# Loads of resident weights moved to another DMA queue, and one load moved behind two others

## The chip, the cores and the metric

The kernel runs on one core of a Trainium2 chip. The metric is the device time of one execution in microseconds (us). TensorE (PE in the profile) multiplies matrices; VectorE (DVE), ScalarE (ACT) and GpSimd (POOL) work on tiles; SyncE (SP) issues DMAs. A DMA can be issued by SP or by ScalarE, and stands in the program of the engine that issues it: what comes before it there has been issued before it. In the profile the transfers of SP are on the queue q1 and those of ScalarE on q10; the same 16 DMA engines carry both.

## What is computed

Three parts follow on one another, all in float32, on 8 x 576 = 4608 tokens:

```
q_s = softmax(q, over head_dim);  k_s = softmax(k, over seq)
x = q_s @ (k_s^T @ v)              # 8 batches, 8 heads, 64 wide -> x is [4608, 512]
h = x @ w_in;  g = h * sigmoid(h);                 x = g @ w_out     # first MLP, 512 -> 2048 -> 512
h = x @ w_in2; g = h * clip(h + 3, 0, 6) / 6;      out = g @ w_out2  # second MLP
```

## The kernel before

A product of float32 accuracy is made of three matmuls of split operands (a high part and a rest). Most products are also made by a scheme with seven products of half-size blocks instead of eight, so the weights are kept as seven operands, each with its high part and its rest. Such a prepared pair of weight columns is a tile of 1792 KB. It is made once, stored to DRAM in `wd`, and loaded from there by `fill` (line 277).

Tokens go in 9 blocks of 512 (NB), the hidden dimension of 2048 in 8 pairs of 128 columns (NC), so an MLP has 72 steps (PER). There are three long stages:

- **Attention and first MLP**, steps 0 to 71 (`first_cycle`, `cycle`). Weights of w_in come through a ring of two tiles, `ring`. In the last step `keep_in(2, 4, 4)` (line 760) asks for pairs 2 and 3 of the second w_in.
- **Products with the second w_in**, steps 72 to 143 (`step_in`, about 5 us each). All eight pairs stay in SBUF: pairs 0 and 1 in the ring, 2 and 3 in one pool, 4 to 7 in another. `keep_in(4, NC, 6)` (line 1239) asks for pairs 4 and 5 before the first of these steps; `slot` (line 906) asks for 6 and 7 in the steps 0 and 2. All of these tiles are `kin` in the profile. Right behind `keep_in`, `feed()` (line 1245) lets ScalarE issue the load of `st`, raw words of the second w_out, which line 127 (ScalarE) reads in the second of these steps. During these steps the second w_out is prepared, one pair a block.
- **Products with the second w_out**, 72 steps (`step_out`, line 1077 for its matmuls).

The order of the work on each engine is that of the program: it is written out by hand (`manual_schedule`), with no planner.

A step k of the second stage ends with g: `gate` on ScalarE (line 838), `gated` on VectorE (line 845), and the store of the tile g to DRAM, `gd`, on SP's queue (line 852). There are three buffers of g, so `gated` of step k waits until the store of step k - 3 has landed:

```
        x["g"] = g_p.tile([P, 2, TB], F32, tag="gs", name="g2")
    ...
        nc.sync.dma_start(out=gd[u][:, k % 2], in_=x["g"])
```

In the last block of this stage (k = 64 to 71) `last_block(p)` is called at the end of each step: for p = 0 it asks for the first two tiles gt of g (`load_g`, line 939, two steps' g in each), for p > 0 it calls `load_out(p - 1)`, which loads pair p - 1 of the second w_out into the place of the w_in pair that was used up (tiles `ring` for pairs 0 and 1, `kout` for the rest). `load_out(7)` comes after the last step (line 1251). Two steps of the third stage follow, then `load_g(2)`, `load_g(3)` and the forming of operands from g (`make_g`: lines 951, 976, 978); later tiles gt are asked for and formed inside `step_out`. The last load of a pair, of step 7 in the third stage, is so far issued ahead of `load_g(2)`.

Of the kernel before, what the change touches and what calls it, by code (L numbers as in the profile page):

```python
# [29 lines left out]
NC = NF // 2  # L30
# [5 lines left out]
def attention_two_mlps(ctx: ExitStack, tc: tile.TileContext, kqT, kv5, qn, w1, w2, out):  # L36
    nc = tc.nc
# [26 lines left out]
    def f32(ap):  # L64
        return ap.bitcast(F32)
# [91 lines left out]
    wd = {}  # L157
# [80 lines left out]
    def split_out(m, p, get_w):  # L238
        def high():
            wo[m, p] = (  # L240
                w_pool[p].tile([P, 2 * DM], F32R, tag=f"a{p}", name="woh"),
                w_pool[(p - 1) % 9].tile([P, 2 * DM], F32R, tag=f"b{(p - 1) % 9}", name="wol"),
            )
            nc.scalar.copy(wo[m, p][0], get_w())

        def low():
            h, l = wo[m, p]
            nc.vector.tensor_tensor(out=l, in0=get_w(), in1=f32(h), op=ALU.subtract)

        return [(0, high), (1.2, low)]  # L250
# [23 lines left out]
        m, t, p = place(g)  # L274
        fill(ring_tile(g), m, p)

    def fill(r, m, p):
        nc.sync.dma_start(out=f32(r).rearrange("p h s n -> p (h s n)"), in_=wd[m, p])


    un = {}
# [304 lines left out]
    second_in = {}  # L586
    WI = {1: 1, 2: 2, 3: 6, 4: 0, 5: 3, 6: 4, 7: 5}

    def place(g):
        m, r = divmod(g, PER)  # L590
        t, p = divmod(r, NC)
        return m, t, p
# [36 lines left out]
    def layer_out(g, n):  # L629

        m, t, p = place(g)
        j, c = divmod(n, KC)
        if p == 0 and n == 0:
            acc[m, t] = [ps_y.tile([P, 512], F32, tag=f"y{k}", name=f"y{k}") for k in range(KC)]
        y = acc[m, t][c]
        start, stop = p == 0 and j == 0, p == NC - 1 and j == 1
        sl = slice(c * P, (c + 1) * P)
        if whole(g):
            w = raw_out[p][:, j * DM:(j + 1) * DM]
            nc.tensor.matmul(y, lhsT=w[:, sl], rhs=gs[g, j], start=start, stop=stop)  # L640
        else:
            wh, wl = (w[:, j * DM:(j + 1) * DM] for w in wo[m, p])
            gh, gl = gs[g, j][:, 0], gs[g, j][:, 1]
            mm3(y, wh[:, sl], wl[:, sl], gh, gl, start, stop)
        if stop:
            put(m, t, c, y)
# [69 lines left out]
    def cycle(g):  # L716
        A, B_, C = (banks[k] for k in "ABC")
        lo, hi = slice(0, HT), slice(HT, TB)
        m, t, p = place(g)
        n = m * NB + t  # L720
        last = p == NC - 1
        G = lambda k: layer_out(g - 1, k)
        late = g >= LATE
        early = n == 1 and NC - 4 <= p < NC - 2

        cast_out = split_out(0, p, lambda: raw_out[p])

        def side(k):

            run(8 * g + k)  # L730
            if n == 1:
                if early and k == 2:
                    pre.append(prepare_in(p + 2))
                if k < 2:
                    cast_out[k][1]()
                for i in {0: (3, 5), 1: (6,)}.get(k, ()):
                    if len(pre) and p in (NC - 3, NC - 2):
                        pre[0][i][1]()
                        if i == 6:
                            pre.pop(0)  # L740
                if early and k in (2, 3, 5, 6):
                    pre[-1][{2: 0, 3: 1, 5: 2, 6: 4}[k]][1]()
            if late and g > LATE and k < 4:
                pump({NC - 1: (1.2, 0.8, 0.8, 0), 0: (1.2, 1.2, 1.2, 0.7)}.get(p, (2.4, 1.2, 1.2, 0.7))[k], keep=k > 0)
            if p == NC - 2 and k in (6, 7):
                sums_x(n + 1, k - 6)
            if last:
                for i in {1: (1,), 3: (5,), 4: (6, 2), 5: (3,), 6: (7,), 7: (4,)}.get(k, ()):
                    operand_x(n + 1, i)

        if g == LATE:
            attn.close()
            m2_p.append(stack("m2", 1, right, side="right"))
            stream.extend((1, q, 0) for q in range(NC))
            feed(2)
            steps.extend(chain([second(q, 0) for q in range(NC)]))
        if g == PER - 1:
            pump(99)
            right.close()
            keep_in(2, 4, 4)  # L760
        product(g, 1, A[:, lo], True)
        nc.scalar.copy(B_[:, lo], A[:, lo])
        product(g, 5, C[:, lo], True)
        s5 = z_p.tile([P, HT], F32, tag="s5", name="s5")
        nc.scalar.copy(s5, C[:, lo])
        side(0)
        G(0)
        G(1)
        product(g, 6, B_[:, lo], False)
        s2 = z_p.tile([P, HT], F32, tag="s2", name="s2")  # L770
        nc.vector.tensor_tensor(out=s2, in0=B_[:, lo], in1=s5, op=ALU.add)  # L771
        side(1)
        product(g, 2, A[:, lo], False)
        product(g, 3, A[:, hi], False)
        G(2)
        nc.vector.tensor_tensor(out=A[:, hi], in0=A[:, hi], in1=s2, op=ALU.add)  # L776
        ba, bc = bend(g, 0, A), bend(g, 1, B_)
        next(ba)
        side(2)
        product(g, 7, B_[:, lo], False)  # L780
        nc.vector.tensor_tensor(out=B_[:, hi], in0=B_[:, lo], in1=s5, op=ALU.add)
        next(ba)
        G(3)
        side(3)
        G(4)
        product(g, 4, B_[:, lo], False)
        if not early:
            load_w(g + 2)
        for _ in ba:
            pass  # L790
        next(bc)
        next(bc)
        side(4)
        G(5)
        for _ in bc:
            pass
        side(5)
        G(6)
        side(6)
        G(7)  # L800
        side(7)
# [2 lines left out]
    kept, early, mid = (ctx.enter_context(ExitStack()) for _ in range(3))  # L804
    kept_p = {}

    def keep_in(a, b, now):
        q = stack(f"kept{a}", 1, kept, side="right")
        for p in range(a, b):
            kept_p[p] = q  # L810
            second_in[p] = q.tile([P, 2, 7, 2 * P], F32R, tag=f"k{p}", name="kin")
            if p < now:
                fill(second_in[p], 1, p)

    gd = {}
    a2 = {}
# [70 lines left out]
    def beside(k):  # L887
        t, p = divmod(k, NC)
        n = NB + t + 1
        if p == 0 and t < NB - 1:  # L890
            c = [c[1] for c in second(t, 1, add=nc.gpsimd)]
            mag, floor, shift, sign, low, sum_0, sum_1, high_0, low_0, high_1, low_1, keep_0, keep_1 = c
            f = lambda i, part: (lambda: operand_x(n, i, part))
            more = [feed] * (t < NC - 1)
            a2["table"] = [
                [lambda: load_y(n)] * (t > 0) + a2.pop("over", []), [], [mag], [floor], [shift], [sign],
                [low, sum_0, sum_1, f(1, 0)], [f(1, 1), f(2, 0), lambda: sums_x(n, 0, nc.gpsimd)],
                [f(2, 1), lambda: sums_x(n, 1, nc.gpsimd)], [high_1], [low_1, f(3, 0)],
                [f(3, 1), f(5, 0), keep_1, *more], [f(5, 1), f(7, 0)], [f(7, 1), f(4, 0)],
                [f(6, 0), f(4, 1), f(6, 1), high_0], [low_0],  # L900
            ]
            a2["over"] = [keep_0]

        def slot(i):
            if k in (0, 2) and i == 1:
                fill(second_in[6 + k // 2], 1, 6 + k // 2)
            if t < NB - 1:
                for fn in a2["table"][2 * p + i]:
                    fn()
            else:  # L910
                if i:
                    last_block(p)
                for fn in ahead_of_out().get(2 * p + i, ()):
                    fn()

        return slot
# [3 lines left out]
    def load_out(p):  # L920
        if p < 2:
            r = ring_tile(2 * PER + p)
        else:
            r = kept_p[p].tile([P, 2, 7, 2 * P], F32R, tag=f"k{p}", name="kout")
        second_out[p] = r
        fill(r, 2, p)

    out_p = {}
    ORDER = [*range(NB - 2), NB - 1, NB - 2]
# [3 lines left out]
    def load_g(u):  # L933
        t, h = divmod(u, NC // 2)
        if u % 3 < 2:
            raws[u] = out_p["a"].tile([P, 2, 2, TB], F32, tag="gt", name="gt", bufs=2)
        else:
            raws[u] = out_p["b"].tile([P, 2, 2, TB], F32, tag="gt", name="gt")
        nc.sync.dma_start(out=raws[u], in_=gd[ORDER[t] * (NC // 2) + h])
# [40 lines left out]
    def make_g(q):  # L980
        if q % 2 == 0:
            for j in range(4):
                sums_g(q // 2, j)
        form_g(q, 0, 0)
        form_g(q, 1, 0)
        form_g(q, 0, 1)
        form_g(q, 1, 1)
# [165 lines left out]
    with tc.manual_schedule():  # L1153
# [82 lines left out]
            layer_out(PER - 1, k)  # L1236
        weights_1.close()
        load_y(NB + 1)
        keep_in(4, NC, 6)
        sums.close()  # L1240
        up["p"] = stack("in_ps", 1, mid, space=bass.MemoryType.PSUM)
        raw_bufs[0] = 1
# [5 lines left out]
        for k in range(PER):  # L1248
            step_in(k, beside(k))
        step_in(PER, lambda i: None)  # L1250
        load_out(NC - 1)
        mid.close()
        up["p"] = stack("out_ps", 1, mid, space=bass.MemoryType.PSUM)
        step_out(0)
# [2 lines left out]
        out_p["b"] = stack("out_b", 1, mid)  # L1257
        load_g(2)
        load_g(3)
        make_g(2)  # L1260
        make_g(3)
        for q in range(2, PER):
# [55 lines left out]
```

## Time and profile before

| | us |
|---|---|
| median of 3 runs | 1669.71 |
| lowest and highest run | 1666.25, 1675.86 |
| the profiled execution | 1680.23 |
| its span, first to last instruction | 1678.4 |

The profile is of that one execution. TensorE is busy for 96% of the span, VectorE for 71%, ScalarE for 46%, GpSimd for 15%. The mean granted clock of TensorE is 0.99 of full speed. q1 moves 323.49 MB, q10 61.35 MB. In a row of a timeline the first number is the start and the second the length, both in us; a bracket at the end has the idle time of the engine ahead of the instruction and what ended it. A row of an engine with a q (SPq, ACTq) is the issue of a DMA, and its length includes what the issue waited for if several are merged; "x3" are three instructions.

### The profile page before, as it was taken

What the parts mean: (1) busy time and instruction counts of PE and PEld (TensorE: products, weight loads), DVE (VectorE), ACT (ScalarE), POOL (GpSimd) and SP (SyncE); (2) the same over time, 40 slices, a digit from 0 to 9 for tenths busy, and PEclk for the clock granted to TensorE, in tenths of its full rate; (3) what the DMA queues carried; (4) which work ended last, traced back from release to release, by engine and by line L of the source; (5) the groups of instructions that cost most, each with busy time, mean ns of one, the idle gap of its engine ahead of it and who ended that gap; (6) DMA issues with size and microseconds to landing.
All of it is one profiled execution on the core that took longest, in us unless ns stands there. A gap on an engine that the chain in (4) does not pass through costs nothing. (4 is left out here: it accounts for less than half of the span.)

```text
span 1678.4 us, 28093 instructions
## 1 busy us (share of the span) xinstructions
PE 1617.6 (96%) x11112; PEld 1461.3 (87%) x11112; DVE 1194.6 (71%) x1910; ACT 767.0 (46%) x1383; POOL 249.4 (15%) x188
## 2 busy tenths in 40 slices
PE   6999999999999999999999899999999899999998
PEld 4445878888889898988789899999999899999998
DVE  7998686575656647568777577777776587778875
ACT  5544555454444545344444455555554343343332
POOL 2211232222222222200000122222220000000000
PEclk9999999999999999999999999999999899999999
DMA  8589979999899999858888955555558833333332
GB/s 297 188 283 287 241 222 240 264 274 262 211 286 263 246 261 263 232 211 319 298 317 330 367 198 200 195 208 205 201 204 335 331 144 126 127 126 126 126 127 75
DMA packets 90107, 386.62 MB, mean 230 GB/s; under 512 B 21880, under 2 KB 25976, under 8 KB 67960
## 3 DMA queue, kind: packets, MB, share of 16 engines
q1 hardware_dynamic: 77272, 323.49, 61.2%
q10 hardware_dynamic: 12704, 61.35, 10.6%
q8 instruction: 87, 1.43, 0.3%
q14 instruction: 44, 0.36, 0.1%
HBM read 283.90 MB, written 100.90 MB: 229 GB/s over the span
## 5 line engine op out<-in xcount | busy, mean ns | idle before, releaser
L1077 PE MATMUL M<-kout,f 128*128 128x256 f32 x2268 | 273.0, 282 | 2.4 <-DVE f L978 1.9
L1077 PEld LDWEIGHTS M<-kout,f 128*128 128x128 f32 x2268 | 271.4, 190 | 3.2 <-DVE f L978 2.3
L77 PE MATMUL y<-gs,woh 128*128 128x512 f32 x512 | 205.9, 402 | 2.8 <-ACT gs L73 2.8
L78 PE MATMUL y<-gs,woh 128*128 128x512 f32 x512 | 203.4, 397 | 0.2 <-DVE gs L74 0.2
L79 PE MATMUL y<-gs,wol 128*128 128x512 f32 x512 | 201.2, 393 | 0.0
L976 ACT CAST f<-gt 128x1024 fp32r<-128x1024 f32 x72 | 75.6, 1050 | 180.5 <-DVE gt L951 98.9
L77 PE MATMUL B<-o,ring 128*128 128x256 f32 x492 | 142.7, 290 | 14.3 <-DVE s L771 7.6
L74 DVE TENSOR_TENSOR gs<-g,gs 128x512 fp32r<-128x512 f32 x128 | 102.4, 800 | 70.8 <-ACT gs L73 70.0
L79 PE MATMUL B<-o,ring 128*128 128x256 f32 x492 | 139.8, 284 | 0.0
L78 PE MATMUL B<-o,ring 128*128 128x256 f32 x492 | 139.7, 284 | 0.0
L77 PE MATMUL A<-op,ring 128*128 128x256 f32 x444 | 127.2, 286 | 2.2 <-DMA ring<-wd 2.2
L78 PE MATMUL A<-op,ring 128*128 128x256 f32 x444 | 126.0, 284 | 2.4 <-DVE op L578 2.4
L79 PE MATMUL A<-op,ring 128*128 128x256 f32 x444 | 125.8, 283 | 0.0
L619 ACT ACTIVATE g<-A 128x512 f32<-128x512 f32 x72 | 43.0, 598 | 176.3 <-DVE A L776 165.4
L77 PEld LDWEIGHTS B<-o,ring 128*128 128x128 f32 x492 | 93.8, 191 | 31.6 <-DVE s L771 11.8
L79 PEld LDWEIGHTS y<-gs,wol 128*128 128x128 f32 x512 | 97.2, 190 | 21.9
L73 ACT CAST gs<-g 128x512 fp32r<-128x512 f32 x128 | 79.2, 619 | 79.7 <-DVE g L621 78.8
L77 PEld LDWEIGHTS y<-gs,woh 128*128 128x128 f32 x512 | 97.8, 191 | 15.8 <-ACT gs L73 3.0
L978 DVE TENSOR_TENSOR f<-gt,f 128x1024 fp32r<-128x1024 f32 x72 | 88.0, 1222 | 32.2 <-ACT f L976 30.9
L77 PE MATMUL B<-o,kin 128*128 128x256 f32 x324 | 94.5, 292 | 14.5 <-DVE B L862 14.4
L78 PEld LDWEIGHTS y<-gs,woh 128*128 128x128 f32 x512 | 98.0, 192 | 9.4 <-DVE gs L74 0.5
L845 DVE SCALAR_TENSOR_TENSOR g<-a,A 128x512 f32<-128x512 f32 x72 | 49.5, 688 | 75.8 <-ACT a L838 60.8
(224 smaller groups left out, 4219.7 us busy)
## 6 DMA issues: line engine op xcount, KB each, us to landing
ring<-wd SPq DMA_DIRECT2D x66, 1792.0 KB, 10.6
gd<-g SPq DMA_DIRECT2D x72, 512.0 KB, 3.4
gt<-gd SPq DMA_DIRECT2D x36, 1024.0 KB, 4.9
st<-w_dram SPq DMA_DIRECT2D x16, 1024.0 KB, 6.2
st<-w_dram ACTq DMA_DIRECT2D x16, 1024.0 KB, 8.6
wd<-r ACTq DMA_DIRECT2D x16, 1024.0 KB, 5.6
ev<-kv_dram SPq DMA_DIRECT2D x24, 640.0 KB, 9.2
wd<-ring ACTq DMA_DIRECT2D x8, 1792.0 KB, 9.8
```

The lines of the kernel that those rows point to most:

```text
L73: nc.scalar.copy(hi, src)
L74: nc.vector.tensor_tensor(out=lo, in0=src, in1=f32(hi), op=ALU.subtract)
L77: nc.tensor.matmul(o, lhsT=wh, rhs=xh, start=start, stop=False, **kw)
L78: nc.tensor.matmul(o, lhsT=wh, rhs=xl, start=False, stop=False, **kw)
L79: nc.tensor.matmul(o, lhsT=wl, rhs=xh, start=False, stop=stop, **kw)
L619: nc.scalar.activation(out=a, in_=hb, func=AF.Tanh, scale=0.5)
L845: nc.vector.scalar_tensor_tensor(out=x["g"][:, j], in0=x["a", j], scalar=1.0, in1=x["AB"[j]], op0=ALU.min, op1=ALU.mult)
L976: nc.scalar.copy(o[0], src)
L978: nc.vector.tensor_tensor(out=o[1], in0=src, in1=f32(o[0]), op=ALU.subtract)
L1077: nc.tensor.matmul(M[:, h * 2 * P:(h + 1) * 2 * P], lhsT=a, rhs=b, start=p == 0 and h == 0 and e == 0, stop=p == NC - 1 and e == 2, skip_g ...
```

## The change

The fills of pairs 4 to 7 of the second w_in and all fills of the second w_out are issued by ScalarE instead of SP. Pairs 2 and 3 stay with SP, and so do the stores of g, the loads gt and the ring's loads of the first MLP. The load of the last w_out pair moves from behind the last w_in step to behind `load_g(2)` and `load_g(3)`.

```diff
-    def fill(r, m, p):
-        nc.sync.dma_start(out=f32(r).rearrange("p h s n -> p (h s n)"), in_=wd[m, p])
+    def fill(r, m, p, by=nc.sync):
+        by.dma_start(out=f32(r).rearrange("p h s n -> p (h s n)"), in_=wd[m, p])
...
-            keep_in(2, 4, 4)
+            keep_in(2, 4, 4, nc.sync)
...
-    def keep_in(a, b, now):
+    def keep_in(a, b, now, by):
...
-                fill(second_in[p], 1, p)
+                fill(second_in[p], 1, p, by)
...
             if k in (0, 2) and i == 1:
-                fill(second_in[6 + k // 2], 1, 6 + k // 2)
+                fill(second_in[6 + k // 2], 1, 6 + k // 2, nc.scalar)
...
         second_out[p] = r
-        fill(r, 2, p)
+        fill(r, 2, p, nc.scalar)
...
-        keep_in(4, NC, 6)
+        keep_in(4, NC, 6, nc.scalar)
...
         step_in(PER, lambda i: None)
-        load_out(NC - 1)
         mid.close()
...
         load_g(2)
         load_g(3)
+        load_out(NC - 1)
         make_g(2)
```

## Rows read from the trace of the kernel before

**Rows 1.** The page: busy us, share of the span, instructions of each engine.
```profile
PE 1617.6 (96%) x11112; PEld 1461.3 (87%) x11112; DVE 1194.6 (71%) x1910; ACT 767.0 (46%) x1383; POOL 249.4 (15%) x188
```

**Rows 2.** Waits, whole span: who waited for what; us in total, times, longest.
```profile
DVE g L845 <- DMA gd<-g: 15.1, 5, 7.4
```

**Rows 3.** Timeline of TensorE near 940, 959, 1306, 1320 and 1331.
```profile
940.10 0.28 PE L77 MATMUL B<-o,kin 128*128 128x256 f32 x1
...
959.16 0.58 PE L77 MATMUL B<-o,kin 128*128 128x256 f32 x1 [6.25 <-DVE B L862]
...
1306.15 0.58 PE L77 MATMUL B<-o,kin 128*128 128x256 f32 x1 [3.66 <-DVE B L862]
...
1319.62 10.10 PE L1077 MATMUL M<-kout,f 128*128 128x256 f32 x84
1330.22 0.50 PE L1077 MATMUL M<-kout,f 128*128 128x256 f32 x2 [0.51 <-ACT f L976]
...
1331.73 1.58 PE L1077 MATMUL M<-kout,f 128*128 128x256 f32 x8 [1.01 <-DVE f L978]
```

**Rows 4.** Stretches: length, busy us by engine, TensorE's clock, DMA share, GB/s.
```profile
960.00:965.00 5.00, 5.00 (x29) 5.00 (x29) 2.60 (x7) 3.10 (x5) 0.00 (x0) 0.59 0.36 145
...
1296.00:1300.00 4.00, 4.00 (x36) 4.00 (x36) 2.40 (x5) 1.90 (x4) 0.00 (x0) 1.00 1.01 430
...
1306.00:1312.00 6.00, 5.85 (x27) 5.85 (x28) 3.39 (x6) 0.69 (x1) 0.00 (x0) 0.50 1.01 428
...
1332.00:1336.00 4.00, 4.00 (x22) 3.90 (x22) 3.93 (x6) 1.08 (x2) 0.00 (x0) 0.59 0.34 72
```

**Rows 5.** Timeline of SP (issues of DMAs), 930 to 947.
```profile
930.99 2.58 SPq L278 DMA_DIRECT2D kin<-wd  x3
941.35 5.20 SPq L852 DMA_DIRECT2D gd<-g  x2
```

**Rows 6.** Timeline of ScalarE, 929 to 939.
```profile
929.52 0.33 ACTq L101 DMA_DIRECT2D st<-w_dram  x1
930.28 0.36 ACT L824 COPY B<-A 128x256 f32<-128x256 f32 x1 [0.17 <-PE A L79]
...
936.73 1.16 ACT L127 ACTIVATE w<-st 128x1024 f32<-128x1024 f32 x1 [1.64 <-DMA st<-w_dram]
938.17 0.36 ACT L824 COPY B<-A 128x256 f32<-128x256 f32 x1 [0.28 <-PE A L79]
```

**Rows 7.** Timeline of VectorE near 957, 1304 and 1328.
```profile
956.87 0.69 DVE L845 SCALAR_TENSOR_TENSOR g<-a,A 128x512 f32<-128x512 f32 x1 [7.39 <-DMA gd<-g]
...
1304.46 0.69 DVE L845 SCALAR_TENSOR_TENSOR g<-a,A 128x512 f32<-128x512 f32 x1 [2.84 <-DMA gd<-g]
...
1327.67 0.69 DVE L951 TENSOR_TENSOR tg<-gt 128x512 f32<-128x512 f32 x1 [6.02 <-DMA gt<-gd]
```

**Rows 8.** DMA near 969, 970:974, 989, 143: issues to landing; queues' packets, MB, share.
```profile
st<-w_dram ACTq DMA_DIRECT2D x1, 1024.0 KB, 8.6
...
gd<-g SPq DMA_DIRECT2D x1, 512.0 KB, 8.6
...
q10 hardware_dynamic: 213, 1.07, 104.6%
...
gd<-g SPq DMA_DIRECT2D x1, 512.0 KB, 2.6
...
q10 hardware_dynamic: 33, 0.47, 50.2%
```

**Rows 9.** DMA, the issue at 932.03: KB, us to landing.
```profile
kin<-wd SPq DMA_DIRECT2D x1, 1792.0 KB, 19.2
```

**Rows 10.** Timeline of ScalarE, last block, step of 1293.
```profile
1293.03 0.69 ACT L838 ACTIVATE a<-B,half 128x512 f32<-128x512 f32 x1
```

**Rows 11.** Timeline of SP, last block and the step behind it.
```profile
1294.47 0.32 SPq L852 DMA_DIRECT2D gd<-g  x1
...
1314.18 19.84 SPq L939 DMA_DIRECT2D gt<-gd  x4
```

## The prediction

> **What bounds the kernel now.** I read the page first: TensorE is busy for 1617.6 us of a span of 1678.4 [rows 1], so nothing but its idle time and its slow stretches can be won, and 61 us is all the idle time there is. The view of the waits comes second. In it the reader looks for a wait whose releaser the change touches: VectorE's line 845, which writes g, waited 15.1 us in five waits for the stores gd<-g [rows 2]. These stores share SP's queue with the 1792 KB weight loads. The third view is TensorE's timeline, read for its brackets. In the second MLP three places matter, and VectorE's timeline tells what each waits for:
>
> - **Start of the second MLP.** Idle 6.25 us until 959.16 [rows 3]. VectorE waited 7.39 us for a store of g [rows 7], issued at 941.35 behind three loads of resident pairs [rows 5].
> - **End of its last block.** Idle 3.66 us until 1306.15 [rows 3]; VectorE waited 2.84 us for a store [rows 7].
> - **Fifth step of the output product.** Idle 0.51 and 1.01 us near 1331 [rows 3], because the tile gt came only at 1327.67 [rows 7].
>
> After each, the view by stretches shows the granted clock at 0.5 of full speed, the 1.2 GHz level. A matmul then takes twice as long, so a stretch at half speed loses half its length. In 960 to 965 the mean of 0.59 makes 4.1 us at half and 2.05 us lost; in 1306 to 1312, 5.85 busy us at 0.50 lose 2.9; in 1332 to 1336, 0.59 makes 3.28 us at half and 1.6 lost [rows 4]. So the places cost 8.3, 6.6 and 3.1 us, 18 us together: the scope of a change that removes all three.
>
> **The change part by part.** Its intent works only if a transfer on ScalarE's queue does not hold one on SP's queue. The trace shows such a pair in each block: by 968.7 ScalarE has issued a load of st (1024 KB, 8.6 us to landing), and at 969.7 SP issues a store of g. This store took 8.6 us to land too; one with no neighbour, near 989.6, took 2.6. In 970.5 to 974.5 ScalarE's queue q10 had all the busy time of the 16 DMA engines, 104.6%, with the store waiting on q1 [rows 8]. So the transfers were served in the order of issue, over both queues. Against that stands one stretch, 142.6 to 144.8, where two loads of equal size, one on each queue, shared: q10 had 50.2% [rows 8]. I take order of issue, as the case with a store of g behind loads is the one that matters here, and keep sharing as a rival.
>
> The Trainium skill says otherwise (DMA: Bandwidth & Descriptors, section "Queues, rings and completion order"): each DMA engine takes turns between the queues that have work, a packet at a time. By that rule the stores of g would pass the loads. The stretch at 142.6 agrees with it, the one at 970.5 does not; the sum by it is the first rival's.
>
> *Start of the second MLP.* Two loads of kin (pairs 4 and 5) move to ScalarE's queue, and in ScalarE's program they stand ahead of feed(), which loads st. In the trace st is issued at 929.52, ahead of all, and line 127, which reads it, starts at 936.73 after an idle 1.64 us that st's landing ended [rows 6]. Behind line 127 in ScalarE's program stands the copy of line 824, at 938.17 [rows 6], and a product of TensorE needs that copy, at 940.10 [rows 3]. So TensorE hides only about 1.6 us of a later st (940.10 less the copy's end at 938.53).
>
> After the change st comes behind 2 x 1.835 MB. A load of 1792 KB at the 430 GB/s of the stretch 1296 to 1300 [rows 4] takes 4.27 us. Which transfers are served by then is the same set as before (st, yd, xr, two of kin); before, the second kin closed it, issued at 932.03 and 19.2 us later landed, at 951.2 [rows 9]. Now st closes it. If st gets ahead of xr (of st's size, 1.05 MB; at 430, 2.4 us), it lands at 948.8. Then 1.16 us for line 127, 0.36 for the copy and 0.1 for the semaphore: TensorE goes on at 950.4 to 952.8.
>
> The three DMA issues also stand ahead of the copy at 930.28. SP's issue of these three loads took 2.58 us in all [rows 5], st's 0.33 [rows 6]; two and st cost 2.05 us from 929.52, so the copy starts near 931.5 instead of 930.28. TensorE has about 0.2 us to spare there: 1.0 us lost, bounds 0 and 2.
>
> So TensorE runs dry at 941.1 and waits until 950.4 to 952.8: 9.3 to 11.7 us, I take 10.5. The old idle 6.25 goes: all of block 1 is delayed, and the stores then find the queue nearly empty. Clock cost as before. **Sum: 1.0 + 10.5 - 6.25 = +5.25 us.** Bounds: if ScalarE's queue alone were served from 931 (the yd and xr of SP held back), st would land after 8.5 + 2.4 us at 942, the gap would be 2.5 us and the sum -2.75; above, copy 2 and gap 11.7 give +7.5. I take the upper half, as the landing at 951.2 is a row for the same bytes.
>
> The loads of pairs 6 and 7 are needed at steps 6 and 7, more than 15 us later: nothing.
>
> *Last block.* Here q1 is full: 430 GB/s at a busy share of 1.01 [rows 4]. Each step issues one store of g (512 KB) and one w_out pair (1792 KB), the store first, as at 1294.47 [rows 11]. On ScalarE the pair's load will follow line 838 of the same step, which starts at 1293.03 [rows 10]; the store must still wait for that operation and for VectorE. So each load will be issued about 1.4 us ahead of the store that it followed, and in order of issue each store gets one pair more ahead of it: 4.27 us. VectorE has three g buffers and already waits for a store in the last two steps, with no cover left: **+4.27 us**. Bounds: 0, if the store still goes first; +7.7, if the waits, then in three steps, cost two more stretches at half clock (1.7 us each, as near 1334).
>
> The eight issues themselves (0.33 us each, as st's [rows 6]) fall behind line 838, where ScalarE then waits for TensorE in most steps: nothing; with that cover gone, 2.6 us.
>
> *The last pair behind the two gt loads.* SP issued the last w_out pair just ahead of four gt loads, the first at 1314.18 [rows 11]. Taking 1.835 MB from in front brings gt 4.27 us earlier, to about 1323.4. VectorE idled 6.02 us until gt came [rows 7], so its chain moves by as much and TensorE's 1.52 us of idle time and the 1.6 at half clock go: **-3.1 us**. Late next is the last pair itself, landing near 1330; it is read by the eighth step. At 5.06 us a step (two steps, 84 matmuls, in 10.10 us from 1319.62 [rows 3], the third and fourth) that is 1319.6 + 5 x 5.06 = 1345: covered by 15 us. Bounds -3.1 and 0.
>
> **Total:** 5.25 + 4.27 - 3.1 = +6.4 us on the profiled execution (1678.4 span, 1.83 around it, 1680.2), that is 1686.6. This execution was 10.5 us above the median of the runs, 1669.7; the difference carries over: **1676.1 us**, 0.4% slower. About 0.5% (8.3 us) is what can be told from no change, so it may not show.
>
> **Rivals.**
>
> - *The queues share.* Stores of g pass the loads. st is still third on its own queue: SP's 2.1 MB and ScalarE's first 2.1 MB take until 940.8, the other 1.57 MB of kin 3.65 us and st 2.4 to 4, so it lands near 947.6, and the gap is 947.6 + 1.6 - 941.1 = 8.1: +2.9 at the start. In the last block VectorE's wait of 2.84 goes but its operand from ScalarE is ready only 2.05 us sooner; with 0.38 us a step earlier and half of the clock's cost, -3.9. With -3.1: -4.1 us, **1665.6**. For it: 142.6; against: 970.5.
> - *It does what it says*, and st is not late, because the 1.64 us wait ends by another transfer than I think. Then -8.3, -3.9 and -3.1: -15.3, **1654.4**. Against it: the order of the program on ScalarE.
> - *Slower for certain.* Loads that pass the stores spread the wait at the end over three steps, and the clock falls in each: place 1288 to 1312, price 3.4 us more than my sum, +9.8, **1679.5**. It decides as soon as the clock is at half ahead of 1300. For it: near 1331 the clock fell after 1.5 us of idle time; against: the single waits may stay short.
>
> **How the numbers follow.** My forecast 0.42 (own range 1672 to 1680), sharing 0.20, all as meant 0.13, slower for certain 0.20, something else 0.05. Faster by over 0.5% (below 1661.4): 0.13 + 0.05 of sharing + 0.04 = 0.22. Slower (above 1678.1): 0.16 + 0.14 of my own + 0.03 = 0.33. Within: 0.45. The range, 1660 to 1683, takes in the upper bounds of the start and leaves out "all as meant" and little else.
>
> **What would show it.** Right: line 127 in the first block waits about 12 us or more for st; TensorE idles some 10 us near 945; the idle time near 955 for gd<-g is gone; VectorE's waits for gd<-g in the last block are longer; no wait for gt near 1327. Wrong: stores of g landing in under 6 us beside loads on q10, or a short wait at line 127.

## The result and the profile after

The changed kernel takes **1683.26 us**, the median of 8 runs (1678.83 to 1690.57). The kernel before, run beside it, takes 1675.09 (8 runs, 1666.25 to 1678.46). The ratio is 1.0061, with an interval from 1.0042 to 1.0079, which is 7.0 to 13.2 us, 10.2 in the middle (the two medians alone are 8.2 apart). So it is slower, by more than the 6.4 us of the forecast. The forecast of 1676.1 was made from the median of three runs, 1669.71; in these eight the kernel before stands 5.4 us higher, and this part of the distance between 1676.1 and 1683.26 has nothing to do with the change.

The profiled execution took 1684.22 us, its span is 1682.4. Spans differ by what happens long ahead of the change, so I cut both traces at five marks and compare the stretches. The marks are the starts of the last line 655 of the first MLP (an activation on ScalarE), of the 17th and the 64th store gd, of the first matmul of line 1077, and of the first matmul of its seventh step.

| stretch | before | after | difference |
|---|---|---|---|
| start (line 655 to 17th store) | 929.5 to 1029.9: 100.3 | 923.2 to 1029.4: 106.2 | +5.9 |
| middle (to the 64th store) | 238.8 | 238.5 | -0.3 |
| last block (to the first line 1077) | 1268.7 to 1307.6: 38.9 | 1267.8 to 1316.4: 48.6 | +9.7 |
| first six steps of the output product | 35.6 | 30.8 | -4.8 |
| rest | 335.2 | 335.3 | 0.1 |

Each is rounded by itself; from mark one to the end it is 748.9 and 759.2, **+10.3**. In the eleven kernels below and here the middle lies between 238.3 and 238.8 and the rest between 335.1 and 335.3, though the change does not touch them; the start lies between 99.7 and 100.3 in the five kernels that leave it as it was. So I take 1 us as a difference, though each figure is from one execution.

First the page of after: the engines' line and the two queues (packets, MB, share of 16 engines).

```profile
PE 1614.7 (96%) x11112; PEld 1458.1 (87%) x11112; DVE 1188.3 (71%) x1910; ACT 766.3 (46%) x1383; POOL 248.1 (15%) x188
...
q1 hardware_dynamic: 75544, 301.47, 58.5%
q10 hardware_dynamic: 14432, 83.37, 13.5%
```

TensorE's busy time is no larger than before [rows 1]. From mark one on it is 727.5 us in both, so in sum what was lost is idle time, 21.4 us before and 31.7 after. 22.0 MB went from q1 to q10: the 12 loads of 1.835 MB that changed engine.

**Start.** ScalarE's and TensorE's timelines of after near 925 and 945, and the view by stretches (length, busy us of PE, PEld, DVE, ACT, POOL, TensorE's clock, DMA share, GB/s).

```profile
923.21 1.30 ACTq L278 DMA_DIRECT2D kin<-wd  x2
924.54 0.72 ACTq L101 DMA_DIRECT2D st<-w_dram  x1
925.37 0.36 ACT L824 COPY B<-A 128x256 f32<-128x256 f32 x1 [1.57 <-PE C L79]
...
944.09 1.12 ACT L127 ACTIVATE w<-st 128x1024 f32<-128x1024 f32 x1 [13.91 <-DMA st<-w_dram]
```

```profile
925.77 0.39 PE L77 MATMUL B<-o,ring 128*128 128x256 f32 x1 [1.19 <-ACT B L824]
...
945.53 0.58 PE L77 MATMUL B<-o,kin 128*128 128x256 f32 x1 [10.20 <-ACT B L824]
```

```profile
935.00:945.00 10.00, 0.34 (x3) 0.13 (x2) 0.00 (x0) 0.91 (x1) 0.00 (x0) 0.73 1.01 427
...
945.00:950.00 5.00, 4.47 (x22) 4.47 (x23) 3.47 (x7) 1.94 (x5) 0.00 (x0) 0.53 0.55 228
```

The two loads of pairs 4 and 5 now stand ahead of st in ScalarE's program. Line 127 waits 13.91 us for st, where it waited 1.64 [rows 6]; the copy of line 824 stands behind it, and TensorE, which needs the copy, idles 1.19 and 10.20 us. Meanwhile the DMA engines are full (1.01, 427 GB/s). The clock is at half when work resumes. The wait of 7.39 us at line 845 [rows 7] and TensorE's 6.25 [rows 3] are gone.

**Last block.** TensorE's timeline, VectorE's, the stretches, and the waits of after for stores of g (us in total, times, longest).

```profile
1281.51 0.38 PE L77 MATMUL B<-o,kin 128*128 128x256 f32 x1 [2.01 <-DVE B L862]
...
1291.94 0.58 PE L77 MATMUL B<-o,kin 128*128 128x256 f32 x1 [5.26 <-DVE B L862]
...
1314.94 0.58 PE L77 MATMUL B<-o,kin 128*128 128x256 f32 x1 [4.16 <-DVE B L862]
```

```profile
1289.65 0.69 DVE L845 SCALAR_TENSOR_TENSOR g<-a,A 128x512 f32<-128x512 f32 x1 [6.93 <-DMA gd<-g]
...
1295.26 0.69 DVE L845 SCALAR_TENSOR_TENSOR g<-a,A 128x512 f32<-128x512 f32 x1 [1.58 <-DMA gd<-g]
...
1313.26 0.69 DVE L845 SCALAR_TENSOR_TENSOR g<-a,A 128x512 f32<-128x512 f32 x1 [3.34 <-DMA gd<-g]
```

```profile
1290.00:1295.00 5.00, 3.06 (x14) 3.06 (x15) 3.68 (x7) 1.89 (x4) 0.00 (x0) 0.61 0.78 328
...
1315.00:1320.00 5.00, 5.00 (x29) 5.00 (x30) 2.53 (x4) 0.69 (x1) 0.00 (x0) 0.66 0.99 420
```

```profile
DVE g L845 <- DMA gd<-g: 15.5, 5, 6.9
```

The sum of the waits for gd<-g is almost that of before, 15.5 against 15.1 us [rows 2], in as many waits. Whoever reads only this view sees no loss. The waits have moved: the one of 7.39 at the start is gone, and one of 6.93 has appeared in the middle of the last block, where before had none until 1298. Of the wait for gt [rows 7] 1.74 us are left, at 1331.02. TensorE idles 2.01, 5.26 and 4.16 us in the block, 11.4 together; before it was 3.66 [rows 3] and two of 0.76 and 0.38. The clock falls to half at 1291 and again at 1315. The whole block by the view of stretches, before and then after:

```profile
1268.70:1307.60 38.90, 34.10 (x281) 33.44 (x280) 23.68 (x44) 16.22 (x30) 0.00 (x0) 0.97 1.01 404
...
1267.80:1316.40 48.60, 36.99 (x281) 36.19 (x280) 23.68 (x45) 16.27 (x30) 0.00 (x0) 0.92 0.97 368
```

The same 281 matmuls keep TensorE busy for 36.99 us instead of 34.10. So of the 9.7 us about 2.9 are work at the lower clock and 6.8 are idle time.

Why one store takes so long is seen in the issues and in the DMA view. First ScalarE's issues of loads in after, then SP's issues: two loads gt, and two stores, each pair merged in one row:

```profile
1271.12 0.33 ACTq L278 DMA_DIRECT2D ring<-wd  x1
...
1278.34 0.33 ACTq L278 DMA_DIRECT2D ring<-wd  x1
```

```profile
1268.24 1.82 SPq L939 DMA_DIRECT2D gt<-gd  x2
...
1272.82 8.04 SPq L852 DMA_DIRECT2D gd<-g  x2
```

The store that VectorE waited for is the first of these two. A load of ScalarE's was issued 1.7 us ahead of it, another 5.5 us behind; the store had landed when line 845 went on, at 1289.65, which is 16.8 us after its issue. Ahead of it on its own queue stood the two loads gt. The queues in 1276 to 1280 (packets, MB, share):

```profile
DMA packets 152, 1.63 MB, mean 407 GB/s; under 512 B 11, under 2 KB 11, under 8 KB 11
...
q10 hardware_dynamic: 77, 1.10, 72.2%
q1 hardware_dynamic: 75, 0.52, 32.1%
```

No packet has between 512 B and 8 KB, so none is of the store, whose rows are 4 KB: q1 still sent gt, with 32% of the engines. Before, from 1273.8 to 1277, q1 had the engines to itself for these loads (1.15 MB, 104.4%). So the store of after started late because what stood ahead of it was slowed. In 1285 to 1289 it was q1's stores that shared with ScalarE's loads:

```profile
DMA packets 207, 1.72 MB, mean 429 GB/s; under 512 B 21, under 2 KB 21, under 8 KB 114
...
q10 hardware_dynamic: 106, 1.32, 77.9%
q1 hardware_dynamic: 100, 0.38, 23.2%
```

The queues sent about **as many packets each**, 106 and 100. A packet that carries data is one row of a tile: 1792 KB over 128 partitions is 14,336 bytes, 512 KB is 4,096. By the bytes these are 92 rows of the loads (1.32 MB / 14,336) and 93 of the stores (0.38 MB / 4,096); 21 packets are under 512 B and move next to nothing. With equal turns a store gets 4096 / (4096 + 14336) = 0.22 of the rate; the row says 0.23 (23.2 of 101.1).

### The profile page after: what moved, and what is told of

Same layout as the page of the kernel before. It is cut to its first block, busy times and chain, and to the rows that moved or that the text cites. A ratio compares the mean times of both kernels' runs of the same rounds, so it can differ in the third digit from the quotient of the medians.

```text
span 1682.4 us, 28087 instructions
## 1 busy us (share of the span) xinstructions
PE 1614.7 (96%) x11112; PEld 1458.1 (87%) x11112; DVE 1188.3 (71%) x1910; ACT 766.3 (46%) x1383; POOL 248.1 (15%) x188
## 4 chain that ended last, share of the span: by engine, by line
PE 58%; DMA 12%; DVE 9%; ACT 3%; issue 3%; ACTq 0%; POOL 0%; DVEq 0%; SPq 0%; POOLq 0%
PE M L1077 19%; PE y L77 4%; PE y L78 4%; PE y L79 4%; PE B L77 4%; PE B L78 3%; PE B L79 3%; PE A L77 3%; PE A L79 3%; PE A L78 3%; DMA wd<-r 3%; DMA gd<-g 3%; DMA qr<-qr 2%; DMA ring<-wd 2%; ACT a L838 1%
## 5 line engine op out<-in xcount | busy, mean ns | idle before, releaser
L74 DVE TENSOR_TENSOR gs<-g,gs 128x512 fp32r<-128x512 f32 x128 | 96.0, 750 | 71.0 <-ACT gs L73 70.1
L77 PEld LDWEIGHTS B<-o,ring 128*128 128x128 f32 x492 | 93.2, 189 | 31.8 <-DVE s L771 14.5
L73 ACT CAST gs<-g 128x512 fp32r<-128x512 f32 x128 | 79.1, 618 | 75.3 <-DVE g L621 74.5
```

The lines of the kernel that those rows point to most:

```text
L73: nc.scalar.copy(hi, src)
L74: nc.vector.tensor_tensor(out=lo, in0=src, in1=f32(hi), op=ALU.subtract)
L77: nc.tensor.matmul(o, lhsT=wh, rhs=xh, start=start, stop=False, **kw)
```

## The experiments

In the table all figures are from one profiled execution of each kernel, cut at the same marks. "Block and six steps" is the third and fourth stretch together, which is safer where a stall or its half clock lies across the mark between them. From mark one to the end, the difference to before agrees with the ratio within 3 us in every kernel but e4, where it is 5 us off.

| kernel | start | last block | six steps | block and six steps | ratio to before, interval |
|---|---|---|---|---|---|
| before | 100.3 | 38.9 | 35.6 | 74.5 | 1 |
| after | 106.2 | 48.6 | 30.8 | 79.3 | 1.0061 [1.0042, 1.0079] |
| e1_last_pair | 99.7 | 38.1 | 31.9 | 70.0 | 0.9982 [0.9960, 1.0005] |
| e2_kin_act | 106.5 | 38.9 | 35.8 | 74.6 | 1.0030 [1.0010, 1.0050] |
| e3_out_act | 100.3 | 46.6 | 31.7 | 78.4 | 1.0016 [0.9997, 1.0034] |
| e4_st_first | 99.1 | 49.1 | 30.6 | 79.6 | 0.9993 [0.9977, 1.0010] |
| e5_sp_load_first | 100.3 | 42.0 | 29.9 | 71.9 | 0.9985 [0.9967, 1.0003] |
| e6_act_load_later | 100.0 | 41.5 | 32.9 | 74.4 | 0.9993 [0.9975, 1.0011] |
| e8_small_desc | 107.3 | 37.3 | 31.8 | 69.1 | 1.0005 [0.9988, 1.0023] |
| e7_spread | 96.9 | 36.3 | 31.5 | 67.8 | 0.9923 [0.9899, 0.9947] |
| e9_mended | 95.9 | 37.2 | 31.4 | 68.5 | 0.9945 [0.9925, 0.9964] |

**One part alone: e1, e2, e3.** e1 is before with only the last pair moved:

```diff
         step_in(PER, lambda i: None)
-        load_out(NC - 1)
...
         load_g(3)
+        load_out(NC - 1)
```

> Only the last edit: the load of the last w_out pair behind load_g(2) and load_g(3), everything on SP's queue as before. My theory (the pair stood ahead of gt): the wait for gt near 1327 goes, the stage from the first matmul of the output product to its seventh step falls from 35.6 us to 31 or 32, and the whole by 3 to 5 us. Rival (gt is late for the backlog as a whole): the wait stays, no change.

VectorE's timeline of e1:

```profile
1320.40 0.69 DVE L951 TENSOR_TENSOR tg<-gt 128x512 f32<-128x512 f32 x1 [3.10 <-DMA gt<-gd]
```

The wait for gt went from 6.02 us [rows 7] to 3.10, TensorE no longer idles in the first six steps, and its clock no longer falls a second time: 31.9 instead of 35.6, -3.7. The rest of the output product stays at 335.2, so the last pair came in time for the eighth step. In the median the gain is 1.6 us, and its interval holds no change.

e2 is before with the fills of pairs 4 to 7 on ScalarE and nothing else:

```diff
-        keep_in(4, NC, 6)
+        keep_in(4, NC, 6, nc.scalar)
...
-                fill(second_in[6 + k // 2], 1, 6 + k // 2)
+                fill(second_in[6 + k // 2], 1, 6 + k // 2, nc.scalar)
```

> Only the resident pairs 4 to 7 of the second w_in on ScalarE's queue, ahead of the load of st. My theory: line 127 waits some 14 us for st as in the changed kernel, TensorE idles about 10 us near 945, and the stage from the last eviction of the first MLP to the 17th store of g takes 106 us instead of 100.3; the last block and the tail stay at 38.9 and 35.6; in all +6 us. Rival (the loss is all in the last block): no change.

ScalarE's timeline of e2, and TensorE's:

```profile
951.07 1.12 ACT L127 ACTIVATE w<-st 128x1024 f32<-128x1024 f32 x1 [14.20 <-DMA st<-w_dram]
```

```profile
952.52 0.58 PE L77 MATMUL B<-o,kin 128*128 128x256 f32 x1 [10.48 <-ACT B L824]
```

All of the start is here: 106.5 against 106.2 in after, with the same two rows; the last block is untouched. e2 is measurably slower than before, by 1.7 to 8.4 us.

e3 is before with only the fills of the second w_out on ScalarE, the last pair in its old place:

```diff
-        fill(r, 2, p)
+        fill(r, 2, p, nc.scalar)
```

> Only the loads of the w_out pairs on ScalarE's queue, the last of them still ahead of the gt loads. Order of issue (each store gets one pair more ahead of it): the last block 43 us instead of 38.9. Turns by descriptor (a store with 4096-byte descriptors gets 4096 / (4096 + 14336) = 0.22 of the DMA engines beside a pair's load with 14336-byte ones): as in the changed kernel, 48 to 49 us. Tail: 35.6 or longer, as gt is still behind the last pair. Start as before, 100.3.

The waits of e3:

```profile
DVE g L845 <- DMA gd<-g: 23.9, 8, 7.5
```

The last block takes 46.6, +7.7 of the +9.7 in after: most of the loss is here without the other two parts of the change. The wait of 7.5 is in the block, at 1280.47. The 46.6 lies between the 43 expected for order of issue and the 48 to 49 expected for turns. The six steps fall to 31.7 as well, though the last pair was not moved in the program: on q10 it no longer stands ahead of gt on q1. So the gain of the moved pair and the new queue do not add up; either alone brings nearly all of it.

**The start undone: e4.** After, but ScalarE issues st before pairs 4 and 5:

```diff
-        keep_in(4, NC, 6, nc.scalar)
+        keep_in(4, NC, 4, nc.scalar)
...
         feed()
+        for p in (4, 5):
+            fill(second_in[p], 1, p, nc.scalar)
```

> The changed kernel with the load of st issued ahead of the pairs 4 and 5, still on ScalarE's queue. Both theories: line 127 waits under 3 us. Order of issue: the first store of g is behind the pairs' loads again, VectorE waits some 7 us for it and the start takes 99 to 101 us, as before the change. Turns by descriptor: the store shares from the time it is issued, lands in 6 to 9 us instead of 15.4, and the start takes 94 to 97 us. Last block and tail as in the changed kernel, 48.6 and 30.8.

ScalarE's timeline of e4, then the issue of a store of g beside these loads (KB, us to landing):

```profile
929.53 1.14 ACT L127 ACTIVATE w<-st 128x1024 f32<-128x1024 f32 x1 [2.56 <-DMA st<-w_dram]
```

```profile
gd<-g SPq DMA_DIRECT2D x1, 512.0 KB, 12.4
```

Line 127 waits 2.56 us instead of 13.91, and the start takes 99.1 instead of 106.2. That settles the mechanism: st was late because of its place in ScalarE's program. But the store, with the pairs' loads on the other queue, still took 12.4 us, where turns had been expected to give 6 to 9, and TensorE idled 4.27 us for it. It was not alone on its own queue. The load xr that SP issued at 920.95 (KB, us to landing), and q1 in 933.5 to 937, behind the issue of the store at 933.23:

```profile
xr<-yd SPq DMA_DIRECT2D x1, 1024.0 KB, 19.2
```

```profile
DMA packets 136, 1.47 MB, mean 420 GB/s; under 512 B 6, under 2 KB 6, under 8 KB 6
...
q1 hardware_dynamic: 66, 0.52, 35.4%
```

No packet is of the store's 4 KB: q1 still sent xr, which shared the engines with the pairs' loads and landed near 940. Separate queues did not free the stores; they slowed what stood ahead of the store on its own queue. The last block stays at 49.1, as it should. The whole run shows 0.9993, some 5 us less than the stretches of this one execution would give (752.5 against 748.9); I rest only on the stretches that differ from after.

**The last block taken apart: e5, e6, e8.** In after a w_out load is issued ahead of the store of its step *and* on another queue. e5 does the first alone: before, all on SP, the load issued right ahead of the store, and the last pair as in e1.

```diff
-        if p:
-            load_out(p - 1)
...
             gate(k - 1, 1)
+            slot(2)        # load_out(p - 1) in the last block, on SP
...
```

> All loads on SP's queue; in the last block each w_out pair's load stands ahead of the store of g that it followed, and the last pair behind the gt loads. Order of issue costs what was forecast, one pair more ahead of each store: last block 43 us (38.9 before), tail 31 to 32, as on one queue nothing takes turns. If the last block takes 48 us, the queue is no matter and the order alone makes the loss of the changed kernel; if it takes 39, the order does not matter either. Start as before, 100.

VectorE's timeline of e5:

```profile
1292.84 0.69 DVE L845 SCALAR_TENSOR_TENSOR g<-a,A 128x512 f32<-128x512 f32 x1 [2.80 <-DMA gd<-g]
...
1304.01 0.69 DVE L845 SCALAR_TENSOR_TENSOR g<-a,A 128x512 f32<-128x512 f32 x1 [2.14 <-DMA gd<-g]
```

A wait of about 2 to 3 us in each of four steps (1.79, 2.80, 2.05 and 2.14), none long: TensorE idles about 1 us for each, and 2.96 at the end of the block, and the clock does not fall. 42.0, +3.1 in the block and +1.9 against e1 with the six steps; 43 was expected for order of issue.

e6 does the second alone: ScalarE issues the load, but behind the store, in the next step; the last pair as in e1.

```diff
-        fill(r, 2, p)
+        fill(r, 2, p, nc.scalar)
...
             gate(k, 0)
+        slot(3)            # load_out(p - 2) in the last block
...
```

> Start on SP as before. In the last block the loads of the w_out pairs are issued by ScalarE, but about 3 us later in the step, behind the store of g that they followed before; the last pair behind the gt loads. Order of issue alone: the last block takes 38 to 39 us, as before. Turns by descriptor: a load issued behind a store still takes 0.78 of the engines once both are in service, so stores land later than before and the last block takes 42 to 47 us. Tail 31 to 32.

The store issued at 1281.96 in e6 (KB, us to landing):

```profile
gd<-g SPq DMA_DIRECT2D x1, 512.0 KB, 9.7
```

41.5, +2.6 in the block, +4.4 against e1 with the six steps, where 1.0 of it lies (VectorE waits 6.25 us for gt again). Turns were expected to give 42 to 47, order alone 38 to 39: it lies between. The store goes ahead of its step's load here, and still takes 9.7 us beside the load of the step before, issued at 1277.88 and 11.4 us to landing; in before, with such a load ahead of it on the same queue, stores took 7.9 and 8.4.

e8 is after, with each w_out fill cut into two DMAs whose rows are 3,584 bytes instead of 14,336; order, queues and bytes are those of after, and ScalarE issues two DMAs where it issued one.

```diff
...
+        if m == 2:
+            o, i = (a.rearrange("p (a b n) -> p b a n", a=2, b=2) for a in (o, i))
+            for j in range(2):
+                by.dma_start(out=o[:, j], in_=i[:, j])
...
```

> The changed kernel with each w_out pair's load made of two DMAs of the same bytes with rows of 3584 bytes instead of 14336, so a store with rows of 4096 gets 0.53 of the engines beside it instead of 0.22. Turns by descriptor: stores of g in the last block land in 5 to 9 us instead of up to 17, and the last block takes 41 to 44 us instead of 48.6. Order of issue alone: 48 to 49 us. Start 106, tail 31, as in the changed kernel.

The queues of e8 in 1291 to 1293 (packets, MB, share), in the last block:

```profile
q1 hardware_dynamic: 107, 0.44, 53.4%
q10 hardware_dynamic: 115, 0.39, 49.0%
```

And a store of g in the same block (KB, us to landing):

```profile
gd<-g SPq DMA_DIRECT2D x1, 512.0 KB, 7.1
```

Again as many packets each, but the store's are now the larger ones (4096 / (4096 + 3584) = 0.53), and q1 gets 53.4 where it got 23.2. The last block falls from 48.6 to 37.3, below that of before and of the 41 to 44 that I expected, and the ratio from 1.0061 to 1.0005. This is the run that decides: with order, queue and bytes kept, shorter rows are worth 11.3 us. No run splits a load in two and keeps the long rows; that the rows do it, and not the splitting, is read from the shares.

**Two versions: e7 and e9.** e7 leaves everything on SP and moves loads away from the crowded places: pairs 6 and 7 of w_in one step later each, four w_out pairs in the last block instead of seven, the others behind the last store or behind the gt loads.

```diff
-            if k in (0, 2) and i == 1:
+            if k in (1, 3) and i == 1:
...
-        if p:
+        if p in (1, 2, 3):
             load_out(p - 1)
+        if p == NC - 1:
+            load_out(3)
...
-        load_out(NC - 1)
+        load_out(4)
...
         load_g(3)
+        for p in range(5, NC):
+            load_out(p)
```

> All loads on SP's queue, spread out: pair 6 of w_in is asked for after the first store of g and pair 7 after the third (steps 1 and 3 instead of 0 and 2); of the w_out pairs 0 to 2 in the last block as before, pair 3 behind its last step but one, pair 4 behind its last step, 5 to 7 behind load_g(2) and load_g(3). Both theories: with one pair less ahead of it the first store lands 4.3 us sooner: start 97 to 98.5 us instead of 100.3. In the last block no store is behind more than one pair: VectorE does not wait for gd<-g, 35 to 36 us instead of 38.9. Tail 31 to 32, if no pair comes too late (each is due 5.06 us after the one before); in all 8 to 10 us faster than before.

The waits of e7, and TensorE's timeline at the start and at the end of the last block:

```profile
DVE g L845 <- DMA gd<-g: 3.1, 2, 2.2
```

```profile
938.95 0.58 PE L77 MATMUL B<-o,kin 128*128 128x256 f32 x1 [2.96 <-ACT B L824]
...
1296.36 0.38 PE L77 MATMUL B<-o,kin 128*128 128x256 f32 x1 [1.64 <-DVE B L862]
```

The waits for stores fall from 15.1 us [rows 2] to 3.1, and none is left in the start or the last block (the two are at 970.87 and 1052.59). 1660.73 against 1675.59: 0.9923, 8.9 to 16.9 us faster than before. It has the lowest ratio here, though its interval and that of e9 overlap.

e9 is e4 with the rows of every fill on ScalarE cut as in e8:

```diff
...
+        if by is nc.scalar:
+            o, i = (a.rearrange("p (a b n) -> p b a n", a=2, b=2) for a in (o, i))
...
```

> The changed kernel with both faults mended: st asked for ahead of the pairs 4 and 5, and every load of a pair that ScalarE issues made of two DMAs with rows of 3584 bytes. Turns by descriptor: the first store of g lands in 6 to 10 us beside the pairs' loads (12.4 with rows of 14336), the start takes 96 to 98 us, the last block 37 to 38, the tail 31 to 32; in all 6 to 9 us faster than before. Order of issue in the start: 99 us there, as with st first alone.

The first store of e9, which answers to the one of 12.4 us in e4, and ScalarE's timeline:

```profile
gd<-g SPq DMA_DIRECT2D x1, 512.0 KB, 7.0
```

```profile
926.30 0.34 ACTq L101 DMA_DIRECT2D st<-w_dram  x1
926.67 3.72 ACTq L282 DMA_DIRECT2D kin<-wd  x4
```

1665.89 against 1675.84: 0.9945. With st first and short rows the change does what it says, at the start too: 95.9, no fall of the clock. The first store, issued at 941.56, does not find xr ahead of it any more: q1 had no packet from 940.6 to 945. Its price shows in the second row: four issues hold ScalarE for 3.72 us, and TensorE idles 3.22 for the copy behind them.

## Why the prediction was right in its sign and wrong in its size

**Start, +5.25: right.** Line 127 waiting for st, the copy and TensorE behind it, the vanished wait for gd<-g: each was seen. The copy cost 1.19 (1.0), the gap was 10.20 (10.5), the clock cost about what it did before (TensorE is busy for 94.2 us of the stretch, 93.9 before), and the stretch +5.9. e2 has it alone, e4 takes it away. That the gap came out so close is in part luck: it was worked out by order of issue over both queues, and in 930 to 935 of after both queues sent at once, 105 packets with 1.28 MB on q10 and 107 with 0.86 MB on q1.

**Last block, +4.27: the step that failed.** It measured +9.7 in after and +7.7 in e3. The step reads "in order of issue each store gets one pair more ahead of it: 4.27 us", and had chosen order of issue *over* sharing, one or the other. e5 has that order with nothing else, on one queue, and costs +3.1: the term by itself exists, and was put somewhat too large. What the step left out is sharing, which e6 has without the order, +2.6. Sharing was a rival of mine, but as a gain: "stores of g pass the loads". The shares above are those of turns of a packet, and the packets of a store are 3.5 times smaller (14336 / 4096), so a store beside a load is slowed, not freed. So are the loads gt with rows of 8 KB, which stand ahead of the first store on q1. Against e1, which like after has the last pair moved, block and six steps cost +1.9 in e5 and +4.4 in e6 but +9.3 with both in after: more than their sum. In after one long wait brings the clock to half in the middle of the block, at 1291; in e5 it does not fall in the block, in e6 only near its end, at 1298. e8 takes all of it back with shorter rows: block and six steps 69.1, against 70.0 in e1.

I had the numbers for this. The stretch at 142.6 [rows 8] has 33 packets with 0.47 MB, 14.2 KB each: two transfers with equal rows share equally, and this says nothing of a store with rows of 4 KB. (They were not two loads: q1's was the load ring<-wd, q10's the store wd<-ring issued at 139.14.) The rows at 970.5, where the store of g had nothing, were of a transfer that had not yet entered service; they say nothing of the share once it has. Nor was st alone ahead of it: ScalarE had issued a store wd<-r too, at 968.09. In the last block of after the first store waits behind gt, which is slowed by small turns, and then takes small turns itself. The rule of turns that I set aside (the Trainium skill, DMA: Bandwidth & Descriptors, "Queues, rings and completion order") fits the packets of both stretches, 106 to 100 and 107 to 115. What the times hang on is how much a packet carries.

**Rival "slower for certain", +9.8.** Its mark came: the clock was at half ahead of 1300, at 1291, and the +10.2 is close to its +9.8. Its course was another: two long waits of 6.93 and 3.34 us and a short one of 1.58, with the clock falling after two of them and not after all three. By the last block alone it has 4.27 + 3.4 = 7.7 where +9.7 was measured, so the close total is luck in part.

**Last pair, -3.1: right.** e1 has -3.7. After has -4.8, and the clock accounts for the 1.1 more: in before 4.6 us of the half speed from 1305.4 lie behind the mark at 1307.6 (as much as in e1), in after 2.0 of that from 1315.0 (3.4 long) behind 1316.4, and half of the difference is 1.3 us. That is time that moved into the last block, not a gain.

**Total.** 5.9 + 9.7 - 4.8 - 0.3 is 10.5 by the rounded stretches, where +6.4 was forecast. Of the 4.1 more, the last block makes +5.4 and the start +0.7; the six steps take off 1.7 and the middle 0.3.

**What stays open.** Why a store on an empty queue enters service late while the other queue is full is not settled. In before the store of 969.7 had no packet in 970.5 to 974.5 [rows 8]; in e9 the store of 941.56 had none until 945, while q10 sent 103.1%. Rows of 14 KB are not the reason: in the first case 148 of q10's 213 packets were under 8 KB and the other 65 of 8 KB, in the second all were under 8 KB. Here order of issue, as I had read it, is what the rows look like; it is the share behind the entry that I had wrong. Nor is it settled what after's last block would cost if the clock did not fall, since no run has its long wait without that.

## What to carry to other kernels

Here a second queue did not set a small store free from large loads. Where both queues are busy, look at packets and bytes of each queue in the DMA view, work out bytes per packet, and try larger rows for the transfer that someone waits for, or smaller ones for the others. Look also at what stands ahead of that transfer on its own queue: it is slowed too. Before a load is moved to a computing engine's queue, read what stands behind it in that engine's program: a load that is asked for ahead of a wanted one makes the wanted one late (line 127 waited 13.91 us for st, and 2.56 in e4). Where DMA is full for a stretch, moving loads out of it (e7, 0.9923) gained here what moving them to another queue as they were (after, 1.0061) did not.

## What the runs showed that I had not expected

- Two busy queues sent equal numbers of rows (92 and 93; 108 and 107, by the bytes), whatever a row carried: 14,336 bytes against 4,096 gave shares of 77.9 and 23.2%, 3,584 against 4,096 gave 49.0 and 53.4%.
- Cutting rows from 14,336 to 3,584 bytes cost little rate: e8's two queues moved 0.83 MB in 2 us there, 413 GB/s, where long rows had 430 [rows 4].
- The length of one idle time of TensorE did not tell alone whether the clock would fall: 2.96 us at the end of e5's block and 3.22 at the start of e9 left it at full, 2.98 in e1, 2.14 in e8 and 1.98 in e9 at the end of the block brought it to half. In e4's first MLP 3.42 us of idle time, until 879.77, left it at full too.
- Four DMA issues in a row held ScalarE for 3.72 us in e9, 0.93 each, where two took 1.30 in after.
